# A one-core convolution training step: two output stores cut into 112 and 4 rows, and the order of the work behind them written anew

## The chip, the cores and the metric

The kernel runs on one core of one Trainium2 chip. The metric is the device time of one execution in microseconds; smaller is better. Before the change three runs gave 1121.47, 1123.16 and 1124.57 us, so the median is 1123.16 us. One more execution was profiled: it took 1120.9 us, and its trace spans 1119.1 us from the first to the last instruction.

## The reference, cut to what matters

A strided 1-D convolution (31 taps, stride 2, 256 channels in and out, two batches of 16000 steps), a group norm over time per channel, a tanh GELU, and the gradients of all of it:

```python
def _fwd_reference(x, w, gn_gamma, gn_beta):
    B, T, D = x.shape                       # 2, 16000, 256
    K = w.shape[0]; s = 2                   # 31 taps
    L = (T - K) // s + 1                    # 7985
    h = sum over i < K of einsum('blc,cd->bld', x[:, i:i + s * L:s, :], w[i])
    mu  = h.sum over l / L
    var = ((h - mu) ** 2).sum over l / L
    h = (h - mu) / sqrt(var + 1e-5) * gn_gamma + gn_beta
    return gelu(h, approximate=True)

def reference(x, w, gn_gamma, gn_beta, grad_out):
    out, vjp = jax.vjp(_fwd_reference, x, w, gn_gamma, gn_beta)
    return (out, *vjp(grad_out))            # out_0; grads of x (out_1), w (out_2), gamma, beta
```

## The kernel before, in words

**Stages.** The kernel runs F (the convolution, batch 0, then batch 1), G (the input gradient, batch 0, then batch 1) and W (the weight gradient of both batches). The taps are multiplied by a fast scheme: even and odd positions are split on three levels, and each level replaces four products by three (branches A, B_ and C_). Sums of operands that this needs are made on VectorE (DVE), matmuls run on TensorE (PE), ScalarE (ACT) copies and scales PSUM, and DMAs are issued by SyncE (SP) and GpSimd (POOL).

**What sets the order.** Every operation is recorded in a list by `add`, with what it reads and writes. The order in which the recorded operations are emitted is a table of numbers, `SEQUENCE`, written out in the file: each engine gets its share of it in that order, and an instruction waits only for what it depends on. An engine works through its share strictly in turn, so an SP or POOL instruction that waits holds up all later ones of its queue. `load` is the helper that issues a plain DMA, so nearly every DMA stands at line 318 in the profile; transposing DMAs stand at line 323 (`turn`). `load` is called with "POOL" for output stores, but in the stages G0, G1 and W it puts large ones on SP.

**The end of G for batch 1.** G goes over four chunks c of 2048 positions (the last is shorter). For each chunk it works on even and odd output rows in turn (pr 0 and pr 1), each in three branches. The finished rows lie in two SBUF tiles, `HO[0]` and `HO[1]`, with 16 rows of the output on each partition, 8192 bytes. `p_evac` (line 1255) adds the last branch into the tile (line 1267) and issues one store of the tile to `out_1` (line 1270). In the chunks 0 to 2 it covers 128 partitions; in chunk 3 it covers 116.

**What W needs from G.** In `dl_turn` each branch of the gradient is transposed by DMA (`turn`) into one of four small slots, `DNO`, and from there POOL stores it to the DRAM tensors `dld`, two stores of 128 KB to a slot. `d_tile` (line 1442) loads slices of them back for part n of W. W has nine parts, n = 0 to 8; part 0 needs `dld0_0` and `dld1_0`. From the loaded tiles `leaf_d` (line 1625) makes the differences `DL`, by four DVE instructions in part 0 (line 1632: branch A or C_, batch 0 or 1). PE's second set of pair products (`w_pairs`, called at line 1661) reads `DL` of branch A of both batches.

**Shared memory.** All tiles lie in one SBUF array, `arena`, at byte offsets given by hand:

```python
GREG = 127424                                                                 # line 357
HO = [sb(119232, 2, 4, 512), sb(GREG + 16704, 2, 4, 512)]                     # 358
DNO = {True: [...], False: [sb(GREG + o, 2, 2, D) for o in (0, 2048, 25088, 27136)]}      # 364
DL = {(i3, b): sb(146880 + 4608 * (i3 + b), 9, D) for i3 in (A, C_) for b in range(2)}    # 1403
```

With A = 0 and C_ = 2 this gives, in bytes: `HO[1]` 144128 to 152320; the last two `DNO` slots in use, 152512 to 154560 and 154560 to 156608; `DL[A,0]` 146880 to 151488, `DL[A,1]` 151488 to 156096, `DL[C_,0]` 156096 to 160704. So `DL[A,0]` and `DL[A,1]` may be written only when the store of `HO[1]` has read its tile, `DL[A,1]` and `DL[C_,0]` only when POOL's stores from the last slot are done.

Of the kernel before, what the change touches and what calls it, by code (L numbers as in the profile page):

```python
# [238 lines left out]
def conv_stem_kernel(  # L239
# [143 lines left out]
    for t in (*(v.rearrange("p e f -> p (e f)") for l in LL for v in l), S[A].rearrange("p e i f -> p (e i f)")):  # L383
        v = t.rearrange("p (r f) -> p r f", f=XM)[:, :, 256:XM]
# [870 lines left out]
    def p_evac(c, pr, brs, br, lf, ps):  # L1255
        r = {A: 0, C_: 1}
# [569 lines left out]
```

## Time and profile before

| | |
|---|---|
| median of three runs | 1123.16 us (1121.47 to 1124.57) |
| profiled execution, its span | 1120.9 us, 1119.1 us |
| PE busy | 1077.3 us, 96% of the span |
| DVE busy | 968.2 us, 87% |
| ACT, POOL busy | 574.9 us (51%), 130.1 us (12%) |
| chain that ended last, by engine | PE 81%, DVE 9%, DMA 4%, issue 2%, ACT 2% |
| granted PE clock, mean | 0.990 |

A kernel with PE busy for 96% of its span has little idle PE time in all, so the reader looks for where that idle time lies and what follows it. The page's view in 40 slices has one pair of slices in which PE falls to 8 and 5 tenths and the granted clock to 6; it lies at about 810 us, which is where G ends and W begins. The views with a window open that place.

### The profile page before, as it was taken

The page shows a single profiled execution, that of the slowest core. Times are in us where ns is not written, and L with a number is a line of the kernel's source. Part 1 is how long each engine was busy: PE and PEld are TensorE (multiplying, and loading weights), DVE is VectorE, ACT ScalarE, POOL GpSimd, SP SyncE. Part 2 cuts the span into 40 slices and gives each one's busy share as a digit, 9 for nine tenths or more (in the row PEclk, how much of TensorE's full clock was granted, in tenths as well). Part 3 has the DMA queues.
Part 4 walks back from the last instruction along what each step waited for, and adds up shares of the span by engine and source line. Part 5 has one row for each costly group of instructions (what it writes and reads, how often), then busy time and mean ns, then how long its engine had stood idle before and what let it go on. Part 6 is the DMA issues. An engine that isn't in the chain of part 4 may idle for free.

```text
span 1119.1 us, 19141 instructions
## 1 busy us (share of the span) xinstructions
PE 1077.3 (96%) x7688; PEld 752.4 (67%) x7688; DVE 968.2 (87%) x964; ACT 574.9 (51%) x884; POOL 130.1 (12%) x239
## 2 busy tenths in 40 slices
PE   6999999999999989999999999999859999999998
PEld 4888899878787974444444444444548868777885
DVE  6987877889999999989896896887659999889996
ACT  1234434587988579899964556554205303212221
POOL 0000000000001003332242443331100000000000
PEclk9999999999999999999999999999969999999999
DMA  9979899877969789999999888779956668987888
GB/s 228 198 188 246 250 252 274 219 157 170 211 167 213 258 327 264 269 254 261 203 237 209 180 229 188 204 179 264 225 204 181 225 180 255 306 287 258 281 244 209
DMA packets 348785, 256.16 MB, mean 229 GB/s; under 512 B 234306, under 2 KB 315848, under 8 KB 343496
## 3 DMA queue, kind: packets, MB, share of 16 engines
q1 hardware_dynamic: 341592, 236.05, 81.1%
q0 software_dynamic: 7104, 18.89, 6.4%
q8 instruction: 60, 0.98, 0.4%
q14 instruction: 29, 0.24, 0.1%
HBM read 114.62 MB, written 84.45 MB: 178 GB/s over the span
## 4 chain that ended last, share of the span: by engine, by line
PE 81%; DVE 9%; DMA 4%; issue 2%; ACT 2%; SPq 1%; DVEq 0%; ACTq 0%
PE ps L517 34%; PE ps L1150 29%; PE ps L1452 18%; DMA dld<-arena 2%; DVE arena L1417 2%; SPq L318 1%; DMA out_dram<-arena 1%; DVE arena L1096 1%; DMA arena<-in_w_dram 1%; DVE arena L1528 1%; DVE ps L1568 1%; DMA arena<-dld 0%; DVE arena L1544 0%; ACT ps L1182 0%; DVE arena L1524 0%
## 5 line engine op out<-in xcount | busy, mean ns | idle before, releaser
L517 PE MATMUL ps<-arena 128*128 128x256 bf16 (+4 forms) x3464 | 396.6, 278 | 12.0 <-DMA arena<-in_x_dram 5.5
L1150 PE MATMUL ps<-arena 128*128 128x512 bf16 (+1 forms) x1776 | 382.6, 376 | 6.5 <-ACT ps L1182 4.5
L517 PEld LDWEIGHTS <-arena 128*128 128x128 bf16 x3464 | 338.1, 98 | 70.2 <-DMA arena<-in_x_dram 5.8
L1150 PEld LDWEIGHTS <-arena 128*128 128x128 bf16 x1776 | 173.8, 98 | 215.0 <-issue 10.7
L1452 PE MATMUL ps<-arena 128*128 128x256 bf16 (+1 forms) x2448 | 298.3, 285 | 19.5 <-DVE arena L1632 17.2
L1452 PEld LDWEIGHTS <-arena 128*128 128x128 bf16 x2448 | 240.5, 98 | 77.2 <-issue 20.1
L596 ACT ACTIVATE arena<-ps 128x1024 bf16<-128x1024 f32 (+1 forms) x105 | 106.1, 1021 | 162.7 <-PE ps L1452 61.6
L475 DVE TENSOR_TENSOR arena<-arena 128x2064 bf16<-128x2064 bf16 (+7 forms) x131 | 162.7, 1265 | 23.7 <-PE ps L517 22.7
L318 POOL DMA_DIRECT2D dld<-arena x144 | 104.3, 726 | 274.6 <-DMA arena<-arena 222.2
L1096 DVE TENSOR_TENSOR arena<-arena 128x1032 bf16<-128x1032 bf16 (+1 forms) x114 | 90.5, 814 | 2.5 <-PE ps L1150 1.7
L562 ACT ACTIVATE ps<-ps 128x256 f32<-128x256 f32 x89 | 36.7, 412 | 86.2 <-PE ps L517 85.2
L1417 DVE TENSOR_TENSOR arena<-arena 128x4096 bf16<-128x4096 bf16 x30 | 68.4, 2289 | 0.3
L1182 ACT COPY ps<-ps 128x512 f32<-128x512 f32 x84 | 48.1, 574 | 36.0 <-PE ps L1150 32.1
L934 DVE TENSOR_TENSOR arena<-arena 128x2048 bf16<-128x2048 bf16 (+1 forms) x48 | 57.5, 1197 | 2.9 <-ACT arena L937 1.2
L327 POOL MEMSET arena<- 128x104 bf16 (+11 forms) x52 | 11.7, 246 | 404.6 <-DVE arena L475 157.6
L1544 DVE TENSOR_TENSOR arena<-arena 128x2048 bf16<-128x2048 bf16 x44 | 52.9, 1221 | 2.5 <-DMA arena<-dld 1.4
L616 ACT ACTIVATE arena<-ps 128x512 bf16<-128x512 f32 (+1 forms) x64 | 37.0, 582 | 32.7 <-PE ps L517 28.2
L896 DVE TENSOR_TENSOR arena<-arena 128x2048 bf16<-128x2048 bf16 (+1 forms) x40 | 47.7, 1197 | 4.0 <-ACT arena L890 1.7
L1638 DVE TENSOR_TENSOR arena<-arena 128x4608 bf16<-128x4608 bf16 x16 | 40.8, 2554 | 6.9 <-PE ps L1452 6.9
L1378 DVE TENSOR_TENSOR ps<-ps,arena 128x1024 f32<-128x1024 f32 x24 | 29.6, 1232 | 15.2 <-PE ps L1150 14.6
L1560 ACT COPY ps<-ps 128x256 f32<-128x256 f32 x54 | 19.3, 357 | 37.0 <-PE ps L1452 35.9
L927 ACT ACTIVATE arena<-arena,stats 128x1024 bf16<-128x1024 bf16 (+1 forms) x32 | 37.8, 1213 | 1.0 <-DVE arena L934 0.9
(102 smaller groups left out, 818.7 us busy)
## 6 DMA issues: line engine op xcount, KB each, us to landing
arena<-in_x_dram SPq DMA_DIRECT2D x36, 1024.0 KB
arena<-hd SPq DMA_DIRECT2D x40, 512.0 KB
dld<-arena POOLq DMA_DIRECT2D x144, 128.0 KB, 4.2
out_dram<-arena SPq DMA_DIRECT2D x13, 1024.0 KB
arena<-dld SPq DMA_DIRECT2D x18, 640.0 KB
arena<-dld SPq DMA_DIRECT2D x18, 576.0 KB
vl<-arena SPq DMA_DIRECT2D x36, 256.0 KB
arena<-vl SPq DMA_DIRECT2D x9, 1024.0 KB
```

Source lines behind the costliest of these rows:

```text
L318: lambda: e.dma_start(out=out, in_=in_), dma=np_ * ns / 16e3 * 1.03, ns=ns, tp=SH[pk], slack=slack)
L475: lambda: nc.vector.tensor_tensor(out=o, in0=a, in1=b, op=ALU.add))
L517: yield nc.tensor.matmul(ps[:, dh, cs], lhsT=wt, rhs=mv, start=s0, stop=False, skip_group_check=True)
L596: lambda: nc.scalar.activation(out=out, in_=ps, func=ACT.Copy, scale=scale))
L896: add("DVE", dve(nf), [o], [a, b_], lambda: V.tensor_tensor(out=o, in0=a, in1=b_, op=op))
L934: add("DVE", dve(nf), [o], [a, b_], lambda: V.tensor_tensor(out=o, in0=a, in1=b_, op=op))
L1096: lambda: nc.vector.tensor_tensor(out=o, in0=a, in1=b, op=ALU.subtract))
L1150: yield nc.tensor.matmul(ps[:, e, 0:wide], lhsT=lt, rhs=mv, start=s0, stop=False, skip_group_check=True)
L1182: add("ACT", act(512), [o], [i], lambda: nc.scalar.copy(out=o, in_=i))
L1417: add("DVE", dve(4096), [o], [a, b], lambda: nc.vector.tensor_tensor(out=o, in0=a, in1=b, op=ALU.add))
L1452: yield nc.tensor.matmul(ps[:, s, c0:c1], lhsT=lt, rhs=mv, start=s0, stop=False, skip_group_check=True)
L1544: add("DVE", dve(2048), [o], [u, v], lambda o=o, u=u, v=v: nc.vector.tensor_tensor(out=o, in0=u, in1=v, op=ALU.subtract))
```

## The change

Two things are edited. In `p_evac` the store of a finished tile is issued as two stores where its number of partitions is not a multiple of 16: the 116 partitions of chunk 3 go as 112 and 4. Chunks 0 to 2 have 128 partitions and stay one store each. `SEQUENCE` is the same up to about the first operations of batch 1's input gradient (about 601 us in the profiled execution) and is replaced from there to its end; it now has two entries more.

```diff
@@ SEQUENCE, from its 2042nd entry to the end (two rows of some forty that differ)
-2012 2064 2013 2047 2071 2061 2021 2054 2072 2093 2022 2062 2073 2154 2048 2065 2099 2063 2075 2049 2066 2153 2067 2094 2076 249 2069 2057 2098 2095
+2012 2094 2064 2013 2047 2098 2071 2061 2021 2054 2072 2095 2022 2062 2073 2048 2065 2099 2063 2075 2049 2066 2067 2076 2148 2069 2172 2096 2077 249
...
@@ p_evac
             add("DVE", dve(1024, 1), [o], [ps[:], o], lambda: nc.vector.tensor_tensor(out=o, in0=ps[:], in1=o, op=ALU.add))
             if lf == C_:
                 n = P if c < 3 else 116
-                load(out_1[1, 16 * 256 * c:16 * (256 * c + 2 * n), :].rearrange("(p z r) c -> p z (r c)", z=2, r=16)[:, pr],
-                     ho[0:n].rearrange("p e k f -> p (e k f)"), n * 8192, 4096, "POOL", slack=60.0)
+                v = out_1[1, 16 * 256 * c:16 * (256 * c + 2 * n), :].rearrange("(p z r) c -> p z (r c)", z=2, r=16)[:, pr]
+                h = ho.rearrange("p e k f -> p (e k f)")
+                for p0, p1 in ((0, n // 16 * 16), (n // 16 * 16, n)):
+                    if p0 < p1:
+                        load(v[p0:p1], h[p0:p1], (p1 - p0) * 8192, 4096, "POOL", slack=60.0)
```

Lines below `p_evac` stand three further down in the changed file, so line 1632 is 1635 there.

**SP, at the end of G.** The rows from the last loads before part 0 of W on. In the names, `dld0_0` and `dld1_0` are what part 0 loads, `dld0_2` and `dld1_2` are for part 1, `hd` is the stored forward result. Before:

```order
L323 DMA_TRANSPOSE arena_115<-arena_115 128x4x128 x2
L318 DMA arena_115<-dld1_2_87 128x2560
L318 DMA arena_115<-dld0_0_76 128x2560
L318 DMA arena_115<-dld1_0_85 128x2560
L318 DMA out_1_dram<-arena_115 116x4096 x2
L323 DMA_TRANSPOSE arena_115<-arena_115 128x4x128
L318 DMA arena_115<-in_x_dram 128x8x512 x2
```

After the change:

```order
L323 DMA_TRANSPOSE arena_115<-arena_115 128x4x128
L318 DMA arena_115<-hd1_0_64 128x2x1024
L318 DMA arena_115<-dld0_2_78 128x2304
L318 DMA arena_115<-dld1_0_85 128x2560
L318 DMA arena_115<-dld0_0_76 128x2560
L318 DMA out_1_dram<-arena_115 4x4096
L318 DMA out_1_dram<-arena_115 112x4096
L318 DMA out_1_dram<-arena_115 4x4096
L318 DMA out_1_dram<-arena_115 112x4096
L318 DMA arena_115<-dld1_2_87 128x2304
L318 DMA arena_115<-dld1_2_87 128x2560
```

The first 112 rows belong to `HO[1]`, and so does the second 4-row store; the last 112 rows belong to `HO[0]`. The last transpose of G stood behind the output stores and now stands ahead of them, ahead also of a load of `hd` that came later; the two loads of part 0 have changed places, and one load for part 1 went behind the stores.

**DVE, at the same place.** The rows of line 1267 add the last branch into the tiles, lines 1632 and 1635 are `leaf_d`. Before:

```order
L1267 TENSOR_TENSOR arena_115<-ps_119,arena_115 128x2x512 x2
L1528 TENSOR_TENSOR arena_115<-arena_115 128x2048
L1267 TENSOR_TENSOR arena_115<-ps_119,arena_115 128x2x512 x2
L1524 TENSOR_TENSOR arena_115<-arena_115 128x4096
L1632 TENSOR_TENSOR arena_115<-arena_115 128x2304 x4
```

After the change:

```order
L1267 TENSOR_TENSOR arena_115<-ps_119,arena_115 128x2x512 x2
L1531 TENSOR_TENSOR arena_115<-arena_115 128x2048
L1267 TENSOR_TENSOR arena_115<-ps_119,arena_115 128x2x512 x2
L1635 TENSOR_TENSOR arena_115<-arena_115 128x2304
L1527 TENSOR_TENSOR arena_115<-arena_115 128x4096
L1635 TENSOR_TENSOR arena_115<-arena_115 128x2304 x3
```

The first `leaf_d` instruction (branch C_, batch 1) has changed places with the 4096-wide sum. The next three are branch C_ of batch 0, then branch A of batch 0 and of batch 1, in both orders.

**POOL, its last stores to `dld`.** Before:

```order
L318 DMA dld1_7_92<-arena_115 128x2x256
L318 DMA dld1_8_93<-arena_115 128x2x256 x2
L318 DMA dld1_1_86<-arena_115 128x2x256 x2
L318 DMA dld1_7_92<-arena_115 128x2x256
L318 DMA dld1_6_91<-arena_115 128x2x256 x2
```

After the change:

```order
L318 DMA dld1_6_91<-arena_115 128x2x256
L318 DMA dld1_8_93<-arena_115 128x2x256 x2
L318 DMA dld1_7_92<-arena_115 128x2x256
L318 DMA dld1_6_91<-arena_115 128x2x256
L318 DMA dld1_1_86<-arena_115 128x2x256
L318 DMA dld1_7_92<-arena_115 128x2x256
```

The first of the two `dld1_6` stores was the last of all and is now the first of this group; both need the transpose that moved on SP. The first row of `dld1_7` in the second piece is the store from the last `DNO` slot, on which `DL[C_,0]` waits; before it was the second row of `dld1_7`.

94 rows, old and new, of the table SEQUENCE are left out of this document.

## The prediction

> **What bounds the kernel now.** I read the stages in windows first, since the page's 96% for PE is an average. From 600 us on, the part that the change can reach:
>
> ```profile
> core 0: us, PE busy (x) PEld busy (x) DVE busy (x) ACT busy (x) POOL busy (x), PEclk, DMA share, GB/s
> 600.00:808.00 208.00, 205.57 (x997) 97.53 (x996) 164.75 (x191) 108.09 (x151) 63.30 (x110) 1.00 0.87 212
> 808.00:826.00 18.00, 1.06 (x5) 0.55 (x4) 3.65 (x3) 1.94 (x2) 1.44 (x2) 0.56 0.55 93
> 826.00:831.00 5.00, 4.74 (x25) 3.29 (x24) 4.89 (x6) 0.00 (x0) 0.00 (x0) 0.53 0.87 261
> 831.00:887.00 56.00, 56.00 (x516) 50.19 (x514) 55.24 (x35) 22.31 (x30) 0.00 (x0) 1.00 0.70 214
> 887.00:950.00 63.00, 60.83 (x493) 47.89 (x491) 61.57 (x40) 13.51 (x18) 0.00 (x0) 1.00 0.75 227
> 950.00:1116.00 166.00, 165.07 (x1323) 129.11 (x1321) 147.14 (x104) 37.15 (x57) 0.53 (x1) 1.00 0.85 267
> ```
>
> PE is full except in one place: of 208 us before 808 it lacks 2.43, behind 826 it lacks 0.26 + 2.17 + 0.93, but between 808 and 826 it works 1.06 us of 18. That is where G ends and W begins. PE also runs at half clock there and for 5 us behind. Second, from 826 to 950 DVE is as full as PE: 121.70 of 124 us. So W's first half is paced by when DVE starts as much as by PE.
>
> Next the waits and, as start, length and work, the chain around this place:
>
> ```profile
> DVE arena L1632 <- DMA dld<-arena: 17.6, 1, 17.6
> PE ps L1452 <- DVE arena L1632: 17.2, 2, 16.9
> ```
>
> ```profile
> 798.68 23.50 DMA dld<-arena
> ...
> 823.63 2.63 DVE arena L1632 x2
> 826.26 0.04 issue
> 826.30 60.95 PE ps L1452 x538
> 887.25 5.24 DMA arena<-dld
> ...
> 948.00 1.23 DVE arena L1528
> ```
>
> and the engines' own rows in order of time:
>
> ```profile
> 795.92 2.05 SPq L318 DMA_DIRECT2D arena<-dld  x2
> 800.33 0.86 SPq L318 DMA_DIRECT2D out_dram<-arena  x2
> 801.24 8.07 SPq L323 DMA_TRANSPOSE arena<-arena  x1
> 823.10 1.44 POOL L318 DMA_DIRECT2D dld<-arena  x2 [23.69 <-issue]
> 800.17 2.29 DVE L1524 TENSOR_TENSOR arena<-arena 128x4096 bf16<-128x4096 bf16 x1
> 803.37 1.36 DVE L1632 TENSOR_TENSOR arena<-arena 128x2304 bf16<-128x2304 bf16 x1 [0.91 <-DMA arena<-dld]
> 822.35 3.89 DVE L1632 TENSOR_TENSOR arena<-arena 128x2304 bf16<-128x2304 bf16 x3 [17.62 <-DMA dld<-arena]
> 825.03 1.01 PE L1452 MATMUL ps<-arena 128*128 128x256 bf16 x4 [16.94 <-DVE arena L1632]
> ```
>
> PE stands still for 16.94 us because `leaf_d` is late. DVE's second `leaf_d` (branch C_, batch 0) waits 17.62 us for POOL's store from the last `DNO` slot, issued at 798.68 and landed at 822.18. The third and fourth (branch A) wait for the store of `HO[1]` as well, since they write over it; the profile names one waker, but both waits end here. That both DMAs land so late has one cause, in the DMA columns:
>
> ```profile
> 800.00:802.00 2.00, 2.00 (x21) 1.80 (x19) 2.00 (x2) 1.29 (x5) 0.00 (x0) 1.00 0.97 398
> 806.00:808.00 2.00, 2.00 (x20) 1.72 (x18) 0.00 (x0) 0.00 (x0) 0.00 (x0) 1.00 0.24 102
> 810.00:812.00 2.00, 0.00 (x0) 0.00 (x0) 0.00 (x0) 0.07 (x1) 0.00 (x0) 0.56 3.05 107
> 818.00:820.00 2.00, 0.00 (x0) 0.00 (x0) 0.00 (x0) 0.00 (x0) 0.00 (x0) 0.50 0.26 106
> 820.00:822.00 2.00, 0.00 (x0) 0.00 (x0) 0.00 (x0) 0.00 (x0) 0.00 (x0) 0.50 0.23 69
> 822.00:824.00 2.00, 0.00 (x0) 0.00 (x0) 1.65 (x2) 0.00 (x0) 0.90 (x2) 0.50 0.00 1
> ```
>
> Only the two stores of 116 partitions move here, 2 x 116 x 8192 = 1.90 MB, at 106 GB/s with a share of 0.25 to 0.26. A quarter of 16 engines is 4; ahead of them the same engines moved 398 GB/s at a share of 0.97. So a store of 116 partitions runs on 4 engines: 1.90 MB at 106 GB/s is 17.9 us, which ends at about 821 and so began at about 803.1.
>
> The Trainium skill, DMA: Bandwidth & Descriptors, section on why a DMA increments its semaphore by 16, says that such a DMA uses the largest number up to 16 that divides the slowest dimension: 4 for 116, 16 for 112, 4 for 4. For 116 this trace agrees (0.25); no run here shows 112 yet.
>
> **The change part by part. The stores.** At the rate of 16 engines (398 GB/s) the 112 rows of `HO[1]`, 0.92 MB, take 2.3 us. The 4-row store behind it puts one 8 KB row on each of 4 engines, at 106/4 = 26.5 GB/s 0.3 us; the 4 rows of `HO[0]` ahead of it, 0.3 us more, go while the earlier loads drain. Landing follows the last byte by at most 822.18 - 821 = 1.2 us. Beginning at 803.1 as before, `HO[1]` is free at 803.1 + 2.3 + 0.3 + 1.2 = 806.9. The upper bound lets the other 112 rows share the engines (+2.3): 809.2. Two further issues on SP cost 0.43 each by the row of two in 0.86; behind them on SP stand loads for part 1, which PE needs over 20 us later.
>
> **POOL and the transpose.** SP's transpose of 8.07 us, stuck behind the stores, moves ahead of them, so POOL's last pair no longer waits 23.69 us. The store on which the second `leaf_d` waits goes out fourth of seven at 0.72 us each (1.44 for two), and no longer shares its engines with 18 us of stores. I take it as landed before 805; its cover is DVE's own queue, below. If that cover goes, each us costs one.
>
> **DVE's queue.** New order: first `leaf_d`, the 4096-wide sum, second, third, fourth. The first needs a load that SP issued second of two in 2.05 us and now issues first, so it starts between 803.37 and at most 1.7 earlier (2.05 less one issue of some 0.3), 801.7. Then 1.36 + 2.29 + 1.36 = 5.0 us lie ahead of the third `leaf_d`: it can start at 806.7 to 808.4. With the store at 806.9 I take 807.0, against 823.63: DVE moves up by 16.6 us. PE, whose previous work ends at 808.1, takes the first 4 matmuls at 807.0 + 1.36 = 808.4 and goes on when the fourth is done, at 809.7 (2.63 for the two). Some 1.1 us of idle remain of 17.2.
>
> **The clock.** PEclk is 0.53 in 826 to 831, so the PE work of 825.03 to 830.7 took about 2.7 us too long. The chain, though, runs on DVE from 892 to 949, and at its beginning DVE lost only this much to PE:
>
> ```profile
> 892.56 2.36 DVE L1544 TENSOR_TENSOR arena<-arena 128x2048 bf16<-128x2048 bf16 x2 [1.36 <-DMA arena<-dld]
> 896.12 4.09 PE L1452 MATMUL ps<-arena 128*128 128x256 bf16 x36 [1.58 <-DVE ps L1568]
> ```
>
> The load that it waits for was released by PE's work up to 887.25. So of 2.7 us DVE can pass on between 0 and its 2.3 us of idle time from 826 to 950; I take 1.4. The clock has no reason to fall after 1.1 us of idle: the gap of 1.58 us at 896.12 left PEclk at 1.00 in its window.
>
> The Trainium skill, TensorE: Matmul & The Clock Gate, section on the clock gate, gives a free-running window of about 3.4 us for both falling and rising. By it a remaining idle time beyond 3.4 us would bring half clock back for one to two windows, an estimate of 1.7 to 3.4 us lost; here the mean of 0.56 in 810 to 812 puts the fall at 810.2, 2.1 us behind PE's stop at 808.1, which agrees with a window that runs freely.
>
> **The rest of the new order.** Elsewhere the matmuls and sums are the same, in slightly other turns. It can gain at most the idle PE time left, 2.43 + 2.17 = 4.6 us plus crumbs, and can lose as much again where a hand-over comes late; those are of the size of 1.58. One is visible: in part 4 a product moves behind four others, so ACT's copy out of PSUM comes just before part 5 reuses the bank, for one copy:
>
> ```profile
> L596 ACT ACTIVATE arena<-ps 128x1024 bf16<-128x1024 f32 (+1 forms) x105 | 106.1, 1021 | 162.7 <-PE ps L1452 61.6
> ```
>
> I take 0 in all, with the ends at 4 gained (most of the 4.6) and 3 lost (three such copies).
>
> Sum: 16.6 + 1.4 + 0 = 18.0 us. The profiled execution took 1120.9, which gives 1102.9; it lies 2.3 us below the median 1123.16, so on the scale of the median I forecast **1105 us**.
>
> **The rivals.** *Partial (1108 to 1115).* The spread falls short or a DMA lands late. With 8 engines (212 GB/s) `HO[1]` takes 4.3 instead of 2.3, free at 808.9: 1.9 us dearer, and sharing with `HO[0]` 4.3 more. If the split changed nothing, 0.92 MB at 106 GB/s is 8.7 us, free at 813.3: DVE moves up by 10.3 us, without the clock's part, 1113. The load of `hd` now ahead of part 0's loads, 0.5 MB, costs up to 1.3. For it: DMA share is 0.97 at 800, so everything queues. Against: 398 GB/s was measured a few us earlier on the same engines with 128 partitions. 0.20.
>
> The same page of the Trainium skill, section on rules for kernel authors, says that two transfers of disjoint partition halves serialize and are not worth making. By this rule the split gives nothing, the case of 1113; but its reason is that both halves already use 16 engines, and the row at 806 shows a quarter.
>
> *Better (below 1101).* The new order also fills the 4.6 us of gaps and DVE passes on all 2.3. For it: DVE has 43 us free before 808. Against: the sums of W's parts stand there in the same places. 0.05.
>
> *Eaten (1120 to 1126).* DVE is the pace from 826 to 950; if loads for W come later relative to it, the gain is lost again. Needs 15 us or more from loads. Against: DMA share is 0.70 and 0.75 there. 0.02.
>
> *Slower.* One mechanism: POOL works strictly in turn, and the first of its last seven stores now needs the transpose that was stuck. If that transpose again lands late, all seven wait, among them the fourth, for the second `leaf_d`. With 4 x 0.72 us of issue and the page's 4.2 us to landing,
>
> ```profile
> dld<-arena POOLq DMA_DIRECT2D x144, 128.0 KB, 4.2
> ```
>
> it is slower than before once the transpose lands after 822.35 - 7.1 = 815; at 820 it would be 1128. For it: the 23.69 us of POOL. Against: what held the transpose stood ahead of it on SP and now stands behind. 0.03.
>
> The forecast has 0.70. Together: faster 0.95, same 0.02, slower 0.03, where faster and slower mean more than 0.3%, about what a measurement of this kernel can tell from no change (the three runs spread over 0.28%). The range reaches from all idle time and all of the clock won (some 24 us, 1099) to the case in which the split changes nothing (1113) and a little more: 1099 to 1114.
>
> **What would show it.** In the profile after: at the end of G a DMA share near 1 and over 300 GB/s for about 5 us in place of 0.25 for 18; `leaf_d` (line 1635) waiting under 3 us; PE's gap there under 3 us; PEclk 1.0 behind it; part 0's products starting at about 808 to 810. A share of 0.5 would mean 8 engines. It would be wrong if `leaf_d` still waited 10 us or more, if the largest wait were POOL for a transpose, or if PE had new gaps of several us after 830 that sum to the gain.

## The result, and the profile after

The changed kernel takes **1109.83 us** (median of 8 runs, 1107.01 to 1111.23), the kernel before, run beside it, 1121.88 us (8 runs, 1114.82 to 1124.57): a ratio of 0.9892, with a 95% interval from 0.9869 to 0.9914. It is faster by 12 us, not by the forecast 18. The range of 1099 to 1114 holds it.

The profiled execution took 1107.89 us, with a span of 1106.1; before it was 1120.9 and 1119.1. The stages in windows, in the columns of the prediction's first table:

```profile
core 0: us, PE busy (x) PEld busy (x) DVE busy (x) ACT busy (x) POOL busy (x), PEclk, DMA share, GB/s
600.00:790.00 190.00, 184.74 (x831) 83.17 (x846) 146.80 (x177) 105.16 (x144) 59.85 (x106) 0.99 0.86 211
790.00:808.00 18.00, 17.95 (x122) 11.76 (x121) 17.23 (x15) 5.24 (x9) 2.88 (x4) 1.00 0.75 252
808.00:812.00 4.00, 3.47 (x31) 2.81 (x29) 2.08 (x2) 2.12 (x3) 0.00 (x0) 1.00 0.76 234
812.00:831.00 19.00, 17.95 (x162) 15.68 (x162) 18.96 (x15) 3.00 (x3) 0.00 (x0) 1.00 1.08 284
```

and, while the stores move:

```profile
805.00:809.00 4.00, 4.00 (x39) 3.58 (x38) 2.77 (x2) 0.05 (x1) 0.00 (x0) 1.00 0.96 299
```

The hole of 18 us with 1.06 us of work is gone, and so is the half clock; the DMA share at the end of G is 0.96 in place of 0.25. The first row, though, now lacks 5.26 us of PE's work in 190, where 2.43 was missing in 208 before, and its clock is 0.99. The rows of PE, DVE and SP around the boundary, as start, length and work, with the idle time ahead and its releaser in brackets:

```profile
800.23 10.64 PE L1455 MATMUL ps<-arena 128*128 128x256 bf16 x96
811.33 0.60 PE L1455 MATMUL ps<-arena 128*128 128x256 bf16 x4 [0.46 <-DVE arena L1635]
812.60 3.22 PE L1455 MATMUL ps<-arena 128*128 128x256 bf16 x28 [0.67 <-DVE arena L1635]
800.62 3.56 SPq L318 DMA_DIRECT2D out_dram<-arena  x4
800.68 2.35 DVE L1267 TENSOR_TENSOR arena<-ps,arena 128x1024 bf16<-128x1024 f32 x2
802.95 1.35 DVE L1635 TENSOR_TENSOR arena<-arena 128x2304 bf16<-128x2304 bf16 x1
806.41 1.36 DVE L1635 TENSOR_TENSOR arena<-arena 128x2304 bf16<-128x2304 bf16 x1
809.92 2.63 DVE L1635 TENSOR_TENSOR arena<-arena 128x2304 bf16<-128x2304 bf16 x2 [2.15 <-DMA out_dram<-arena]
```

The second `leaf_d` (806.41) waits for nothing, the third and fourth wait 2.15 us for the store of `HO[1]`, and PE stands still for 0.46 + 0.67 = 1.13 us. But everything here stands 2.8 us further back than forecast, since the last addition into `HO[1]` (L1267) ends at 803.03 and not at 800.26.

With the rows of PE's last products in both profiles (before first, then after), the span falls into four stretches:

```profile
1059.81 55.35 PE L1452 MATMUL ps<-arena 128*128 128x256 bf16 x443
```

```profile
1059.75 40.03 PE L1455 MATMUL ps<-arena 128*128 128x256 bf16 x300
```

| stretch | before, us | after, us | difference |
|---|---|---|---|
| start to the end of PE's work ahead of the stall | 808.10 | 810.87 | +2.8 |
| PE's stall until its next product | 16.9 | 0.5 | -16.5 |
| from there to PE's last product (1115.16, 1099.78) | 290.1 | 288.5 | -1.7 |
| PE's last product to the end of the span | 3.9 | 6.3 | +2.4 |

The stall went as forecast. What is missing are 2.8 us lost ahead of it and 2.4 us lost at the very end. Both are stretches in which the change moved only the order.

### The profile page after: what moved, and what is told of

It reads as the page before. It is cut to its first block, busy times and chain, and to the rows that moved or that the text cites. A ratio compares the mean times of both kernels' runs of the same rounds, so it can differ in the third digit from the quotient of the medians.

```text
span 1106.1 us, 19120 instructions
## 1 busy us (share of the span) xinstructions
PE 1074.6 (97%) x7643; PEld 751.6 (68%) x7688; DVE 967.1 (87%) x964; ACT 575.5 (52%) x884; POOL 129.1 (12%) x239
## 5 line engine op out<-in xcount | busy, mean ns | idle before, releaser
L1182 ACT COPY ps<-ps 128x512 f32<-128x512 f32 x84 | 47.9, 573 | 36.2 <-PE ps L1150 31.5
L975 ACT ACTIVATE arena<-arena,stats 128x1024 bf16<-128x1024 bf16 x16 | 19.4, 1236 | 32.0 <-DMA arena<-hd 32.0
```

Of the source, the lines that this page charges most:

```text
L1182: add("ACT", act(512), [o], [i], lambda: nc.scalar.copy(out=o, in_=i))
```

## The experiments

All times are medians; each ratio is to the kernel before, run on the same chip in the same session (1122.1 to 1122.7 us there). "The changed kernel" is the one just shown, with ratio 0.9892; it was not run again beside these variants, so comparisons with it go by the ratios, and by the profiles.

### The split alone, and the order alone

The old order with the split:

```diff
  the change's code at line 1267 (two stores for each of the two)
- SEQUENCE: the new table
+ SEQUENCE: the old table, each 4-row store right behind its 112-row store
```

> The old order, word for word, with only the two 116-partition stores cut into 112 and 4 rows. What is asked: how much of the 12 us is the split alone, and did the new order help or cost. Theory (the split alone ends the stall, and the new order lost time in two places, 2.8 us in the second batch's input gradients and some 2 us after the last matmul): the stall of 16.9 us falls to 1 to 3 us as it did in the changed kernel, and neither loss is there, so 1121.9 - 17 = about 1104 to 1106, that is 4 to 6 us faster than the changed kernel. Rival (the new order was needed as well: in the old one a transpose stands on SP's queue behind the stores, issued 801.24 to 809.31, and two POOL stores wait for it): the weight gradient's first part waits for those, 1110 to 1114.

Measured: 1103.59 us (1103.18 to 1106.05, 5 runs), ratio 0.9828 (0.9811 to 0.9846). Its interval lies wholly below the changed kernel's (0.9869 to 0.9914): **the split alone is faster than the whole change**. In its profile:

```profile
798.38 10.64 PE L1455 MATMUL ps<-arena 128*128 128x256 bf16 x96
810.50 0.60 PE L1455 MATMUL ps<-arena 128*128 128x256 bf16 x4 [1.47 <-DVE arena L1635]
806.55 5.16 DVE L1635 TENSOR_TENSOR arena<-arena 128x2304 bf16<-128x2304 bf16 x4 [3.17 <-DMA arena<-dld]
802.85 1.51 SPq L323 DMA_TRANSPOSE arena<-arena  x1
```

PE's stall falls to 1.47 us with the old order too. The transpose behind the stores, 8.07 us long before, takes 1.51 with nothing but the stores changed, so its length came with the whole stores. All four `leaf_d` now wait for part 0's load (`arena<-dld`), no longer for a store.

The new order with whole stores:

```diff
  SEQUENCE: the new table, without the two 4-row steps
- two stores each of 112 and 4 partitions
+ one store each of 116 partitions, as before
```

> The new order, word for word, with the stores left whole at 116 partitions. What is asked: does the new order alone end the stall. Theory (the stores' 4 of 16 engines are the cause): the last product block needs HO[1]'s store, issued first at about 803.1. If the engines serve HO[1]'s store ahead of HO[0]'s, it lands after half of their 17.9 us, at 803.1 + 2.8 + 8.7 + 0.3 = about 815, where the changed kernel had it at 809.8: 5 us more and a piece of half clock, 1115 to 1118. If the two stores share the engines, it lands at about 824 as before, and the time is 1123 to 1127: slower than the kernel before by the new order's own losses. Rival (the new order itself ends the stall, the split is worth nothing): 1110, as the changed kernel.

Measured: 1116.96 us (1114.84 to 1121.59, 9 runs), ratio 0.9951 (0.9934 to 0.9968), inside the expected 1115 to 1118. In its profile, SP, DVE and PE, and then the DMA columns of one window:

```profile
804.04 0.68 SPq L318 DMA_DIRECT2D out_dram<-arena  x2
816.72 2.63 DVE L1632 TENSOR_TENSOR arena<-arena 128x2304 bf16<-128x2304 bf16 x2 [8.01 <-DMA out_dram<-arena]
818.13 1.01 PE L1452 MATMUL ps<-arena 128*128 128x256 bf16 x4 [6.32 <-DVE arena L1632]
```

```profile
813.00:815.00 2.00, 0.00 (x0) 0.00 (x0) 0.00 (x0) 1.00 (x1) 0.00 (x0) 1.00 0.26 98
```

The share is again 0.26 at 98 GB/s. `leaf_d` waits 8.01 us for `HO[1]`'s store. It runs 12.7 us behind the issue of the two stores, well before the 18 to 19 us that both stores' 1.90 MB take at this rate are over: here the store that was issued first was served first. The order alone gains some 6 us. In it the second `leaf_d` waits for nothing (it runs at 807.36), where before it hung on a POOL store that landed behind both. With the split, that difference has no worth left.

### Which part of the new order costs

The old order up to just past the boundary, the new one behind it:

```diff
  the split stores
- SEQUENCE: the new table
+ SEQUENCE: entries 0 to 2922 of the old table, from 2923 on the new one
```

> The split stores, with the old order up to just past the start of the weight gradient (the first 2923 entries, which hold the same steps in both orders), and the new order from there. What is asked: is it the new order of the input gradients that cost 2.8 us (TensorE's last product of that stage ends at 810.87 in the changed kernel and at 808.10 before). Theory: it is; this kernel is 2.8 us faster than the changed one, about 1107, and as fast as the old order with the split within the 2 us of the end. Rival (that loss is given back in the weight gradient, which VectorE paces): 1109 to 1110, as the changed kernel.

Measured: 1105.21 us (1104.37 to 1105.74, 4 runs), ratio 0.9841 (0.9823 to 0.9859). It is under the changed kernel by 0.51% or 5.7 us; the two intervals, each some 2 us to a side, do not touch. So the new order of the input gradients costs time. How much is less sure: the two profiled spans differ by 2.4 us (1106.1 and 1103.7), and the changed kernel's profiled execution was one of the fastest of its eight.

What the profiles show there. In the changed kernel PE stands still once for 3 us. SP's, ACT's and PE's rows, in order of time, and two windows behind them:

```profile
666.60 6.04 SPq L323 DMA_TRANSPOSE arena<-arena  x2
672.73 1.71 SPq L318 DMA_DIRECT2D arena<-dyd  x1
678.69 1.15 ACT L1035 ACTIVATE arena<-arena,stats 128x1024 bf16<-128x1024 bf16 x1 [3.19 <-DMA arena<-dyd]
679.75 0.58 ACT L1182 COPY ps<-ps 128x512 f32<-128x512 f32 x1
680.38 13.02 PE L1150 MATMUL ps<-arena 128*128 128x512 bf16 x51 [3.01 <-ACT ps L1182]
```

```profile
681.00:683.00 2.00, 2.00 (x7) 0.76 (x6) 0.00 (x0) 2.00 (x3) 0.00 (x0) 0.56 0.60 154
683.00:685.00 2.00, 2.00 (x7) 0.75 (x6) 1.23 (x1) 0.44 (x1) 0.00 (x0) 0.59 0.74 153
```

The same load and activation before the change:

```profile
672.48 0.33 SPq L318 DMA_DIRECT2D arena<-dyd  x1
677.87 1.16 ACT L1035 ACTIVATE arena<-arena,stats 128x1024 bf16<-128x1024 bf16 x1
```

ACT takes its work in turn. Before, it came to this activation at 677.87 and found the data there. In the new order it is there at 678.69 - 3.19 = 675.50, the load left no sooner (672.73, behind two transposes, with an issue of 1.71 us in place of 0.33), and the copy that PE needs stands behind the activation. PE then works at 0.56 and 0.59 of its clock for 4 us, which is 1.7 us more. Two runs put the copies ahead. First one copy, the actual edit of the table:

```diff
- 2353 2462 2378 2375 2374
+ 2462 2378 2375 2374 2353
```

where 2353 is the activation (L1035) and 2374 the copy (L1182).

> The changed kernel with two neighbours on ScalarE exchanged: the copy of L1182 on which TensorE waited 3.01 us at 677.37 (it ran 679.75 to 680.33) now stands ahead of the activation of L1035, which waited 3.19 us for its load (arena<-dyd, to 678.69) with the copy behind it. Nothing else is moved. Theory (the loss of the new order in the input gradients is this one stall and the 3 us of half clock behind it, 681.4 to 684.4): TensorE's gap falls under 0.7 us, its clock stays at 1.0 there, and the kernel gains 2.8 to 4.4 us: 1105.4 to 1107.0. Rival (the slack behind absorbs it, since VectorE or the transposes set the pace of that stage): 1109 to 1110, with the gap gone all the same.

Measured: 1107.25 us (1106.60 to 1108.46, 4 runs), ratio 0.9862 (0.9843 to 0.9880). The stall did not go, it moved 8 us on, to the next copy of the same queue, and PE's work ahead of the boundary ended no earlier (801.01 + 10.64 = 811.65):

```profile
682.23 1.15 ACT L1035 ACTIVATE arena<-arena,stats 128x1024 bf16<-128x1024 bf16 x1 [3.27 <-DMA arena<-dyd]
688.04 5.99 PE L1150 MATMUL ps<-arena 128*128 128x512 bf16 x28 [3.21 <-ACT ps L1182]
```

So the theory's first sign (a gap under 0.7 us) failed, and the time lies just above its 1105.4 to 1107.0. The ratio is some 3.4 us better than the changed kernel's, but the intervals overlap. Then all three activations of that load's data behind the next two copies:

```diff
  (activations 2353, 2355 and 2354, the rest of the table as in the changed kernel)
- 2353 2462 2378 2375 2374 ... 2381 2355 2463 2383 2385 2354 2382 ... 2392 2386
+ 2462 2378 2375 2374 ... 2381 2463 2383 2385 2382 ... 2392 2386 2353 2355 2354
```

> The changed kernel with ScalarE's three activations of the late load's data (two of L1035, one of L1033) put behind the next two copies of L1182 and two of L596, not behind one copy alone as in the earlier run, where the stall came back 8 us later (3.21 us at 684.8) behind the same load. Theory (nothing but these places on ScalarE's queue makes TensorE stand still there): no wait of TensorE over 1 us between 670 and 700, its clock at 1.0, TensorE some 2 us earlier at 709 than the changed kernel (709.06), and 1107 to 1108.5; the rest of the new order's loss in this stage lies after 705 us and stays. Rival (the load itself is late for the work that needs it, wherever the copies stand): a wait of about 3 us shows up again further on, and the time stays at 1109 to 1110.5.

Measured: 1106.76 us (1106.59 to 1108.63, 4 runs), ratio 0.9859 (0.9837 to 0.9881). PE still waits 2.27 us, behind the three activations that now stand in a row ahead of a further copy, but the clock stays at 1.00:

```profile
687.43 0.57 ACT L1182 COPY ps<-ps 128x512 f32<-128x512 f32 x1
688.06 4.70 PE L1150 MATMUL ps<-arena 128*128 128x512 bf16 x22 [2.27 <-ACT ps L1182]
```

The sign "no wait over 1 us" failed again, while the time came out just under the expected 1107 to 1108.5. The ratio is some 3.7 us better than the changed kernel's, with intervals that just overlap. That ACT's turn makes PE wait at this place is shown, since the wait moves with the steps; what the wait costs the whole kernel is not, and shifting three steps does not remove it.

Two mixed orders asked in which half of the stage the loss lies:

```diff
  the split stores, the new table from entry 2923 on in both
- SEQUENCE: the new table up to there
+ first kernel: the old table for 2500 entries, the new one behind
+ second kernel: the new table for 2500 entries, the old one behind
```

> The split stores; the old order for the first 2500 entries (to about 705 us, past the stall at 677 to 680 of the new order), the new order for all the rest. What is asked: is the new order's loss in the input gradients the one stall behind the late load. By the starts of TensorE's products the new order is 2.5 us ahead of the old one at 667 us, 0.9 behind at 683, 2.0 behind at 705 and 2.8 behind at the stage's end. Theory (the stall and the half clock behind it): this kernel has neither, its last product of the stage ends at 808 to 809, and the time is that of the old order with the new weight gradient, 1105 to 1106. Rival (the loss is spread over the stage, most of it after 705 us): the stage ends at 810 or later, 1107 to 1110.

> The converse: the new order for the first 2500 entries, the old one from there to just past the start of the weight gradient, the new one behind it. Theory (the stall before 705 us is the loss): TensorE stands still for about 3 us at 677 to 680 as in the changed kernel, the stage ends at 810 to 811, and the time is 1108 to 1110. Rival (the loss lies after 705 us): the stage ends at 808, 1105 to 1106.

Measured: the first 1107.99 us (1106.20 to 1108.82, 4 runs), ratio 0.9867 (0.9854 to 0.9881); the second 1108.59 us (1107.41 to 1113.25, 5 runs), ratio 0.9883 (0.9865 to 0.9900). Neither theory holds alone. The second kernel has the stall, here 4.04 us, and loses as expected. The first does not have it and still lies some 3 us above the kernel with the whole old stage, with intervals that just touch; by its time and by the stage's end it is the rival's case. But PE's work ahead of the boundary ends at 812.2 in the first and 813.2 in the second, later than in either whole order. A mixed order has a seam, and in the first a new wait stands 10 us behind it:

```profile
715.43 40.26 PE L1150 MATMUL ps<-arena 128*128 128x512 bf16 x180 [0.73 <-ACT ps L1182]
```

So these two runs do not prove that the new order itself loses as much behind 705 us; in which half it loses stays open. The profiles of all kernels say how much it is in sum. PE's work ahead of the boundary ends at 810.3 to 811.9 in the five with the new order throughout (mean 811.3), and at 808.1 to 811.4 in the seven with the old one (mean 809.4): 2 us on average, with a scatter of 3 us among profiles of one order. The 2.8 of the one pair is within that.

### The end of the kernel

> The split stores; old order up to the first 2923 entries, the new one from there to entry 3109 (about 925 us), the old one to the end. What is asked: does the new order's end cost 2 us. In the profiles of the kernels that end in the new order (the changed kernel, the whole stores in the new order, the old input gradients with the new weight gradient, the copy put ahead) 6.0 to 6.3 us pass from TensorE's last product to the end of the span; in the two that end in the old one (before, and the old order with the split) 3.9 and 4.3. In the new one the last transposes of SP's queue end 4.7 us before the last product, in the old one 7.2 us, and ten stores stand behind them. Theory (it is that queue): the tail is 4.0 to 4.4 us here, and the time 1103 to 1104, 1.5 to 2 us under the kernel that differs only behind entry 3109 (1105.2). Rival (the tail is set by what the products before it left, or the old end loses on TensorE what it gains in the tail): 1105 to 1106.

```diff
  the split stores, the old table up to entry 2922
- SEQUENCE: from 2923 on the new table
+ SEQUENCE: from 2923 to 3108 the new table, from 3109 on the old one
```

Measured: 1104.71 us (1103.98 to 1107.06, 4 runs), ratio 0.9844 (0.9830 to 0.9857). From PE's last product to the end of the span 4.2 us pass, as expected, but the time, between the theory's and the rival's, is that of the kernel it was to beat (0.9841): the profiled execution ended its work ahead of the boundary 2.8 us later than that one with the same order there. Then the same end on the changed kernel:

```diff
  the changed kernel
- SEQUENCE: the new table
+ SEQUENCE: the new table up to entry 3108, from 3109 on the old one
```

> The changed kernel with the old order from entry 3109 (about 925 us) to the end: the converse place of the earlier run, on the new order's input gradients. Theory (SP's queue at the end costs the new order 2 us): from TensorE's last product to the end of the span 3.9 to 4.4 us where the changed kernel has 6.3, and 1107.5 to 1108.5. Rival (TensorE ends later by what the tail is shorter): the tail is 4 us too, and the time 1109.5 to 1110.5.

Measured: 1107.87 us (1106.05 to 1110.32, 5 runs), ratio 0.9867 (0.9843 to 0.9891). The tail is 4.4 us. Over the profiles of this study it is 3.9 to 4.4 us with the old end and 5.6 to 6.3 with the new one, without an overlap. That the new end is longer behind the last product by 2 us is shown; that the whole kernel gains these 2 us from the old end is not, since both differences in time lie within their intervals. What the tail consists of, SP's queue in the changed kernel and in the split with the old order:

```profile
1093.87 1.23 SPq L323 DMA_TRANSPOSE arena<-arena  x1
1095.19 7.44 SPq L318 DMA_DIRECT2D out_dram<-arena  x10
```

```profile
1088.91 4.00 SPq L323 DMA_TRANSPOSE arena<-arena  x3
1093.01 8.52 SPq L318 DMA_DIRECT2D out_dram<-arena  x10
```

The last ten stores begin 4.6 us ahead of the last product (1099.78) in the new order and 6.9 us ahead of it (1099.91) in the old one. Their issue ends 2.9 us behind it against 1.6. DVE's last sum ends at 1100.24 in the changed kernel, and SP issues its last store only 2.0 us later, at 1102.2; with the old input gradients and the new end it is 1.6. In four kernels with the old end (before, the split with the old order, and the two mixed ones of this section) SP issues it 0.3 to 0.4 us behind that sum. So in the new end SP's queue is late by itself, by most of the 2 us.

### What the number of partitions sets

The old order with other cuts of the 116 partitions (the order of the first experiment, one line of code changed):

```diff
- for p0, p1 in ((0, n // 16 * 16), (n // 16 * 16, n)):
+ for p0, p1 in ((0, n if n == P else 104), (n if n == P else 104, n)):
```

> The old order with the stores cut into 104 and 12 partitions, where the first experiment had 112 and 4 (1103.6). What is asked: is it the number of partitions that sets how many DMA engines serve a store. Theory (a store of n partitions is spread over the largest of 16, 8, 4 engines whose number divides n: 116 was served by 4 of 16 at 106 GB/s): 104 gets 8 engines and 12 gets 4, so 1.70 MB move at some 212 GB/s, 8 us from 803 to 811 at a DMA share near 0.5 for that work, where 112 and 4 moved 400 to 450 GB/s; the last product block starts 1 to 4 us later than at 809.1, and the time is 1104 to 1108. Rival (any cut of the store gives it more engines, since the parts run side by side): as 112 and 4, 1103 to 1104.

Measured: 1104.18 us (1103.69 to 1105.25, 4 runs), ratio 0.9836 (0.9821 to 0.9851), the same as 112 and 4. The mechanism that was expected (8 engines, share 0.5) is wrong. While the stores move:

```profile
803.50:807.50 4.00, 4.00 (x39) 3.58 (x38) 2.88 (x3) 0.00 (x0) 0.00 (x0) 1.00 0.80 299
```

0.80 of 16 is 13, and 13 divides 104. Two further cuts put the rule to the test, with 110 and with 113 in the same line:

> The old order with the stores cut into 110 and 6 partitions, which tells two rules apart. Theory (the largest divisor not over 16): 110 = 10 x 11 goes to 11 engines, a DMA share near 0.69 and some 290 GB/s while the stores move, about 6.2 us for both, no stall to speak of: 1103 to 1106. Rival (the largest power of two that divides it): 2 engines, 53 GB/s, 34 us for both stores: 17 us to the first, 1118 to 1140.

> The old order with the stores cut into 113 and 3 partitions. In the run with 104 and 12 the DMA engines' share was 0.79 to 0.87 while the stores moved, not the 0.5 that was expected: 13 of 16 engines, not 8. A rule that fits all three cuts seen (116 by 4 engines, 112 by 16, 104 by 13) is that a store of n partitions goes to as many engines as the largest divisor of n that is not over 16. 113 is prime: by that rule one engine moves each 0.93 MB store, at a quarter of the 106 GB/s that four gave, so 35 us each and 70 for both, and the last product block, which waits for the first of them, starts some 33 us later than at 808: 1135 to 1140, and up to 1175 if it waits for both. Rival (a store of more than 104 partitions that is no multiple of 16 gets four engines whatever its number): the same stall as before the change, 1120 to 1124.

Measured, one run each and so without an interval: 110 and 6 took 1108.47 us, 113 and 3 took **1168.54 us**. The windows, 110 first, in two us ahead of which nothing else had been issued since 809.2:

```profile
811.00:812.00 1.00, 0.38 (x4) 0.19 (x2) 0.04 (x1) 0.58 (x1) 0.00 (x0) 1.00 0.62 254
812.00:813.00 1.00, 0.00 (x0) 0.00 (x0) 1.00 (x1) 1.00 (x2) 0.00 (x0) 1.00 0.74 254
```

```profile
810.00:840.00 30.00, 0.00 (x0) 0.00 (x0) 0.00 (x0) 1.38 (x2) 0.00 (x0) 0.55 0.07 27
```

A mean of 0.68 at 254 GB/s fits 11 engines (0.69) and not 2 (0.13), and 254/11 and the 299/13 of the cut at 104 are both 23 GB/s for an engine. That run lies 2 to 5 us above the expected; in its profile the work ahead of the boundary ended late (811.38, against 809.02 with 112 and 4) and PE stood for 1.99 us. With 113, a prime, 0.07 at 27 GB/s is one engine (0.0625). PE's two stalls there, and the wait of DVE behind the second:

```profile
842.23 1.01 PE L1455 MATMUL ps<-arena 128*128 128x256 bf16 x4 [32.82 <-DVE arena L1635]
879.27 20.91 PE L1455 MATMUL ps<-arena 128*128 128x256 bf16 x167 [27.42 <-DVE ps L1571]
875.72 2.36 DVE L1547 TENSOR_TENSOR arena<-arena 128x2048 bf16<-128x2048 bf16 x2 [28.68 <-DMA out_dram<-arena]
```

The first is `leaf_d` behind the first store, as worked out (33 us); the second is DVE behind the other one, which the 1135 to 1140 had not counted and the 1175 had. The Trainium skill, DMA: Bandwidth & Descriptors, section on why a DMA increments its semaphore by 16, states the rule as the largest number up to 16 that divides the slowest dimension. The runs agree with it for 104, 110, 113 and 116 (0.80, 0.68, 0.07, 0.26), and for 112 the old order with the split shows a share of 1.03 at 422 GB/s in 803 to 809, other transfers included, so that 16 engines fit but are not singled out:

```profile
803.00:809.00 6.00, 6.00 (x56) 5.26 (x54) 2.83 (x3) 0.21 (x1) 0.00 (x0) 1.00 1.03 422
```

## Why the prediction was right and wrong, point by point

**The cause of the stall: right.** The stores of 116 partitions ran on 4 of 16 engines; the order alone kept the share of 0.26, the split ended it, and a cut into 113 and 3 makes it worse than before. One reading was too strong: "both waits end here". With whole stores in the new order `HO[1]` came free 12.7 us behind the issue, which before the change would be about 813 (800.33 + 12.7, an estimate). So what held `leaf_d` to 822 was POOL's store, and `HO[1]` most likely was free long before.

**"The stores" and "DVE's queue": right in mechanism and size, wrong in place.** The forecast had `HO[1]` free 806.9 - 800.26 = 6.6 us behind the last addition; measured are 809.92 - 803.03 = 6.9 us until `leaf_d` runs. PE's idle time was to be 1.1 us and is 1.13. The point in time, 807.0, was wrong by 2.9 us, since all of it hangs on the last addition into `HO[1]`, which the sum left at its old place. How the 6.9 us divide into start, transfer and landing is not shown: the sum took 398 GB/s, and 805 to 809 shows 299. "POOL and the transpose" at nothing: right, the second `leaf_d` waits for nothing.

**"The clock", 1.4 us: too much.** With the old order and the split, PE takes 289.4 us from its restart at 810.50 to its last product at 1099.91, where before it took 290.1; with 104 and 12 it was 289.8, with 110 and 6 289.3. So 0.3 to 0.8 of the 2.7 us were won. In the changed kernel this stretch got shorter by 1.7, of which about 1 us is the new order's: it is 288.5 and, with the old input gradients, 288.9.

**"The rest of the new order", taken as 0: the step that failed.** It was bounded at 4 gained and 3 lost, by the idle time left and by hand-overs "of the size of 1.58". It lost 2 us on average (2.8 in the profile shown) ahead of the boundary and 2 (2.4 in the profile shown) behind the last product, and gained about 1 in between. One hand-over was twice as dear as the 1.58, 3.01 us, and drew 1.7 us of half clock after it. The end of the kernel, where SP's queue was late, was not looked at for the new order at all.

**The sum.** In the profiles 16.5 + 1.7 - 2.8 - 2.4 = 13.0 us, against 18.0. The 18.0 are near the worth of the split: without the new order it measured 1122.73 - 1103.59 = 19.1 us. In part that is luck: in the profile of the split with the old order, the slowest of its five runs, the stall got shorter by 15.5 us and the stretch behind it by 0.7, 16.2 against the sum's 18.0.

**The rivals.** "Partial" (1108 to 1115) holds the measured time, for a reason that it did not name: the spread over the engines did not fall short. Its case of 1113, in which the split gives nothing, did not come either, since the split alone gained 19.1 us. A loss by the new order was named in "eaten", for loads of W, and in "slower", for POOL's queue; as far as the traces show it, it came ahead of W over ACT's queue and at the end over SP's.

**What would show it.** The DMA share near 1 (0.96, with 299 GB/s where over 300 had been named), a PE gap under 3 us, the clock at 1.00 behind it and `leaf_d` waiting under 3 us all came. The products of part 0 started at 811.3, not by 810. The last sign, "new gaps of several us after 830", looked in the wrong direction: the gap lay ahead of the boundary.

The best of all kernels measured is the split with the old order, at 0.9828 (0.9811 to 0.9846). The old order with 104 and 12, and the two that take parts of the new weight gradient, lie within its interval.

## What to carry to other kernels

Before a store or load is given a number of partitions that is no multiple of 16, read the DMA share while it moves: here 4 more partitions in the same transfer cost 19 us, and in one run a cut at the prime 113 took 65 us more than the cut at 112. Where a change joins a sharp edit with a re-planned order, cost the two apart, and put no zero for the order without reading, on each queue that works in turn, which copy now stands behind which late load, and what stands last in the queue that ends the kernel.

## What the runs showed of the hardware that was not expected

- SP's queue stood with the stores. With 113 partitions on one engine the four store issues took 49 us of SP's queue, against 3.56 in the changed kernel, so that SP issued nothing else meanwhile:

```profile
801.63 49.02 SPq L318 DMA_DIRECT2D out_dram<-arena  x4
```

- The clock fell after work had resumed. In the changed kernel PE stopped at 677.37 and worked again from 680.38, the window of 679 to 681 still shows 1.00, and the half clock stands in 681 to 685. The half clock so lasted (0.44 + 0.41) x 2 / 0.5 = 3.4 us, by the two windows shown above. The same happened after gaps of 3.01, 3.04 and 4.04 us in three other kernels, again for 3.4 us each, but not after the 3.21 us that ended at 688.04, behind which the clock stayed at 1.00. So near 3 us the length of a gap alone does not decide. The Trainium skill, TensorE: Matmul & The Clock Gate, section on the clock gate, speaks of a free-running window of about 3.4 us and lets the clock fall after at least one idle window. The 3.4 us of half clock agree with the length of the window, but gaps of 3.01 and 3.04 us are shorter than it and were followed by the fall all the same. That such gaps can fall differently into a free-running window is a possible reason; no run here was made to test it.
